# Idle TensorE products placed piece by piece in the PSUM tiles of an attention and MoE kernel

## The chip, the cores and the metric

The kernel runs on one core of a Trainium2 chip. The metric is device time in microseconds (us), the median of three runs. Five queues of instructions matter: TensorE (PE; its weight loads are PEld), VectorE (DVE), ScalarE (ACT), GpSimd (POOL) and SyncE (SP), which issues the DMAs. Each engine takes its instructions in the order in which the program lists them, and waits on semaphores that other engines count up.

## The reference

Eight batches of eight heads, 576 positions of 64 elements. For each head: `scores = q k^T / 8`, plus a decay that is the difference of cumulative sums of `log(clip(f))`, a causal mask, a softmax, and `attn @ v`. The heads of one position are then set side by side as 512 numbers (4608 tokens), and each token goes through `h = x @ w_in` (1024 wide), `solu = h * softmax(h)`, a layer norm scaled by `g_ln`, and `@ w_out` (back to 512). Everything is float32.

## The kernel before

Work goes by head pairs and halves of the positions (320 and 256), and by tiles of 128 tokens for the MoE part. For a pair, `scores` multiplies q and k into a `ps` tile (L519 plain float32 for the first batch's first half, L521 and L522 in split float32r pieces later), VectorE reduces it with the mask (L526), ScalarE takes the exponential (L529), GpSimd normalizes (L542), `transposes` turns the result on TensorE into `ps_t` (L568), which is copied out as `pth` (L295 on ScalarE, L297 on VectorE), and `values` multiplies with v into `ps_o` (L608). At the start, while the first batch runs, the weights are also unpacked from 8-byte words: `weights` uses a `ps_o` tile as scratch. ScalarE writes it (L376), VectorE combines bits in it (L379) and reads it into the weight buffer (L381).

PSUM is divided by `pool`: two tiles each of `ps`, `ps_t`, `ps_o` (in the listings below `ps_120`, `ps_121`, `ps_t_123`, `ps_t_124`, `ps_o_125`, `ps_o_126`). All instructions are first recorded as operations with a cost in ns and a due time. `Plan.schedule` then plays them through a model of the engines and gives each a planned start; the program is emitted in that order. The model also notes in `held`, for each PSUM tile, the planned spans in which it is taken.

Idle products come in at the emission. When the next planned operation is one of TensorE and starts later than TensorE is planned to be free, the loop at the end (L783 to L794) may put in products of the identity with itself (256 bf16 columns, L793), whose result nobody reads. The number is the planned gap less 100 ns, times 1.2, divided by the planned length of one. It does so only before 140 us of planned time, and only where `spare` finds a tile that is free through the whole planned gap.

Semaphores are set by program order: an instruction that writes a tile waits for every earlier listed instruction on another engine that reads or writes it. An idle product is listed right ahead of the TensorE operation that ends the gap, whatever planned time its tile was chosen for.

Of the kernel before, what the change touches and what calls it, by code (L numbers as in the profile page):

```python
# [37 lines left out]
COLUMN, TRANSPOSE = 0.4525, 109.0  # L38
# [1 line left out]

WI_H, WI_L, WO_H, WO_L = (1, 1, 1, 1), (3, 3, 2, 3), (2, 3, 2, 2, 3, 1, 1, 2), (2, 2, 2, 2, 2, 2, 2, 2)
P_32, X_32 = (1, 2, 1, 1), (2, 2, 2, 2, 1, 1, 1, 2)
FILLED, FILL = 140.0, 1.2
LANES = 8
WAIT = (0.0, 90.0, 60.0, 60.0, 0.0)


class Op:
# [3 lines left out]
class Plan:  # L52
# [30 lines left out]
    def schedule(self):  # L83
        free, wire, order, gone, self.held = [0.0] * 5, 0.0, [], {}, {}
        port, half_clock, worked, lanes = 0.0, True, 0.0, [0.0] * LANES
        todo = [[] for _ in range(5)]
        for o in self.ops:
            o.left, o.ready, o.users = len(o.deps), 0.0, []
            for d in o.deps:
                d.users.append(o)  # L90
            if not o.left:
                todo[o.eng].append(o)
        best = [None] * 5
        stale = set(range(5))
        for _ in self.ops:
            for e in stale:
                ready = []
                for o in todo[e]:
                    r = max(o.ready, free[e], port if o.port else 0.0)
                    if o.take:  # L100
                        if not self.pools[o.take[0]]:
                            continue
                        r = max(r, min(self.pools[o.take[0]])[0])
                    ready.append((r, o))
                best[e] = None
                if ready:
                    t = min(r for r, _ in ready) + WAIT[e]
                    best[e] = min((x for x in ready if x[0] <= t), key=lambda x: (x[1].due, x[1].seq))
            t, o = min((x for x in best if x), key=lambda x: x[0])
            stale = {PE, ACT, DVE, POOL, o.eng}  # L110
            todo[o.eng].remove(o)
            if o.take:
                place = min(self.pools[o.take[0]])
                self.pools[o.take[0]].remove(place)
                self.place[o.take] = place[1]
            if o.eng == SP:
                t = max(t, lanes.pop(0))
                free[SP] = t + 620.0
                wire = max(wire, t + 600.0) + o.ns
                o.end = max(t + 1900.0, wire + 1300.0)  # L120
                lanes.append(o.end)
            else:
                ns = o.ns
                if o.eng == PE:
                    if t < FILLED * 1e3:
                        half_clock = False
                    elif t - free[PE] > 1500.0:
                        half_clock, worked = True, 0.0
                    if half_clock:
                        ns *= 2.0  # L130
                        worked += ns if o.dense else 0.0
                        half_clock = worked < 3500.0
                free[o.eng] = t + ns
                o.end = t + ns
                if o.port:
                    port = o.end
                if o.tail:
                    wire = max(wire, t + 600.0)
                    o.end = max(t + o.tail, wire + 1300.0)
            after = AFTER[o.eng]  # L140
            for k in o.keys:
                gone[k] = max(gone.get(k, 0.0), o.end + after)
                self.uses[k] -= 1
                if not self.uses[k]:
                    self.pools[k[0]].append((gone[k], self.place[k]))
            for u in o.users:
                u.left -= 1
                u.ready = max(u.ready, o.end + (0.0 if u.eng == o.eng != SP else after + (90.0 if u.eng == PE else 0.0)))
                if not u.left:
                    todo[u.eng].append(u)  # L150
                    stale.add(u.eng)
            if o.take:
                self.held.setdefault((o.take[0], self.place[o.take]), []).append([t, 1.0e9])
            for k in o.keys:
                if not self.uses[k]:
                    self.held[k[0], self.place[k]][-1][1] = gone[k]
            order.append((t, o))
        return order

    def spare(self, a, e):  # L160

        for k, spans in self.held.items():
            if all(y <= a or x >= e for x, y in spans):
                return k

# [15 lines left out]
def tile_kernel(ctx: ExitStack, tc: tile.TileContext, qk, v, f, w_in, w_out, g_ln, out):  # L183
# [14 lines left out]
    plan = Plan(s=2, t=2, o=2)  # L198
# [585 lines left out]
    with tc.manual_schedule():  # L784
        busy = 3200.0
        for t, o in plan.schedule():
            if o.eng == PE:
                place = plan.spare(busy, t) if busy + 200.0 < t < FILLED * 1e3 else None
                if place:
                    p, n = place  # L790
                    dst = ps[n] if p == "s" else ps_o[n] if p == "o" else ps_t[n].rearrange("p c n -> p (c n)")
                    for _ in range(int(FILL * (t - busy - 100.0) / (256 * COLUMN))):
                        nc.tensor.matmul(dst[:, :256], blank[:, :P], blank, start=True, stop=True)  # L793
                busy = max(busy, o.end)  # L794
            o.fn()
# [40 lines left out]
```

## Time and profile before

| | us |
|---|---|
| median of 3 runs | 807.3 |
| lowest, highest | 806.41, 811.13 |
| the profiled execution | 804.66 |
| its span on the core | 802.8 |
| TensorE busy | 790.1 (98%) |
| mean granted TensorE clock | 0.994 |

Times in rows are us from the start of the span. A timeline row has start, length, engine, line, operation, out<-in, and in brackets the idle time of the engine just before with what ended it by the profile. Matmul rows overlap by their pipelined ends, so the distance from one start to the next is the cost of one. [...]

### The profile page before, as it was taken

To read this page: it belongs to the slowest core of one execution; us is meant where nothing else is said; L and a number is where in the kernel's file an instruction comes from. 1 tells how busy PE (TensorE), PEld (TensorE's weight loads), DVE (VectorE), ACT (ScalarE), POOL (GpSimd) and SP (SyncE) were. 2 spreads that over 40 slices of the span, in tenths; PEclk is the share of its full clock that TensorE was granted. 3 is DMA by queue.
4 is the path that set the end of the run, shared out by engine and by line. 5 is a ranking of instruction groups with operands and counts; after the bars stand their busy time and mean duration, and the time that the engine had idled before them with its cause. 6 is when DMAs were issued, how large, how long until landed. Compare 5 with 4: busy or idle time off the path is not lost.

```text
span 802.8 us, 15984 instructions
## 1 busy us (share of the span) xinstructions
PE 790.1 (98%) x4924; PEld 675.7 (84%) x4924; DVE 590.5 (74%) x1865; ACT 554.5 (69%) x1373; POOL 459.9 (57%) x668
## 2 busy tenths in 40 slices
PE   8799999999999999999999999999999999999998
PEld 6567889888888888888888888888888888888886
DVE  5698888987777787777777787777777787765233
ACT  6677588877777776777777776767777776764433
POOL 6476677876654565657555565657644656432230
PEclk9799999999999999999999999999999999999999
DMA  7767688886553554556544555555544554100000
GB/s 249 217 174 210 170 212 201 217 212 170 150 125 92 128 150 130 146 146 150 136 103 110 139 137 146 147 136 142 134 105 123 135 137 111 32 14 14 27 27 27
DMA packets 64213, 106.96 MB, mean 133 GB/s; under 512 B 11200, under 2 KB 25792, under 8 KB 63360
## 3 DMA queue, kind: packets, MB, share of 16 engines
q1 hardware_dynamic: 64128, 105.95, 50.1%
q8 instruction: 39, 0.64, 0.3%
q14 instruction: 46, 0.38, 0.2%
HBM read 39.11 MB, written 10.03 MB: 61 GB/s over the span
## 4 chain that ended last, share of the span: by engine, by line
PE 93%; DVE 2%; ACT 1%; DMA 1%; issue 1%; POOL 1%; SPq 0%; POOLq 0%; DVEq 0%; ACTq 0%
PE ps_o L608 15%; PE ps_t L568 11%; PE hps L648 8%; PE hps L649 8%; PE hps L650 8%; PE ps_o L703 8%; PE ps_o L704 8%; PE ps_o L705 8%; PE ps L521 6%; PE ps L522 6%; PE ps_t L692 4%; PE ps L793 2%; PE ps_t L793 1%; PE ps L519 1%; PE ps_o L793 1%
## 5 line engine op out<-in xcount | busy, mean ns | idle before, releaser
L542 POOL TENSOR_SCALAR p<-p,ri 64x64 f32<-64x64 f32 (+4 forms) x320 | 174.3, 558 | 123.4 <-DVE ri L538 53.4
L529 ACT ACTIVATE p<-p,nm 128x320 f32<-128x320 f32 (+4 forms) x320 | 178.9, 560 | 72.8 <-DVE nm L526 68.3
L576 DVE TENSOR_TENSOR ptl_f32r<-ps_t,pth_f32r 128x384 fp32r<-128x384 f32 (+3 forms) x272 | 138.9, 519 | 31.5 <-ACT pth_f32r L295 28.9
L526 DVE CUSTOM_DVE_ANT_0 p<-ps,mask 128x320 f32<-128x320 f32 (+4 forms) x320 | 132.7, 423 | 35.2 <-PE ps L522 21.5
L295 ACT ACTIVATE pth_f32r<-ps_t 128x384 fp32r<-128x384 f32 (+3 forms) x272 | 121.8, 461 | 34.3 <-PE ps_t L568 31.2
L568 PE MATMUL ps_t<-ident,p 128*128 128x128 f32 x800 | 130.9, 274 | 0.0
L648 PE MATMUL hps<-wi_h,xh 128*128 128x512 f32 x288 | 122.3, 425 | 0.0
L703 PE MATMUL ps_o<-wo_f32r,zh 128*128 128x512 f32 x280 | 118.5, 423 | 0.0
L568 PEld LDWEIGHTS ps_t<-ident,p 128*128 128x128 f32 x800 | 98.4, 140 | 23.5 <-issue 2.9
L650 PE MATMUL hps<-wi_h,xl 128*128 128x512 f32 x288 | 113.6, 394 | 0.0
L649 PE MATMUL hps<-wi_l,xh 128*128 128x512 f32 x288 | 113.6, 394 | 0.0
L704 PE MATMUL ps_o<-wo_f32r,zh 128*128 128x512 f32 x280 | 110.9, 396 | 0.0
L705 PE MATMUL ps_o<-wo_f32r,zl 128*128 128x512 f32 x280 | 110.2, 394 | 0.0
L521 PE MATMUL ps<-ks_f32r,qs_f32r 128*64 128x64 f32 (+2 forms) x360 | 107.5, 309 | 0.3 <-DVE nm L526 0.2
L522 PE MATMUL ps<-kz_f32r,qz 128*64 128x64 f32 (+2 forms) x360 | 104.1, 295 | 0.2
L608 PE MATMUL ps_o<-pth_f32r,vs_f32r 128*128 128x128 f32 (+1 forms) x368 | 96.1, 272 | 0.0
L644 POOL TENSOR_TENSOR xl<-xt,xh 128x512 fp32r<-128x512 f32 x36 | 47.5, 1318 | 70.0 <-ACT xh L643 65.9
L695 DVE TENSOR_TENSOR zl<-ps_t,zh 128x512 fp32r<-128x512 f32 x72 | 46.9, 686 | 53.2 <-ACT zh L694 52.6
L674 POOL TENSOR_SCALAR z<-e,st 128x1024 f32<-128x1024 f32 x35 | 41.0, 1172 | 70.2 <-ACT z L670 70.0
L521 PEld LDWEIGHTS ps<-ks_f32r,qs_f32r 128*128 128x128 f32 (+1 forms) x360 | 64.8, 180 | 10.8 <-DVE nm L526 2.7
L608 PE MATMUL ps_o<-ptl_f32r,vs_f32r 128*64 128x128 f32 (+1 forms) x368 | 71.2, 262 | 0.2 <-DVE ri L537 0.2
L608 PEld LDWEIGHTS ps_o<-pth_f32r,vs_f32r 128*128 128x128 f32 x368 | 69.3, 189 | 1.6
(126 smaller groups left out, 1612.2 us busy)
## 6 DMA issues: line engine op xcount, KB each, us to landing
raw<-in_qk_dram SPq DMA_DIRECT2D x64, 288.0 KB
ks_f32r<-hi SPq DMA_DIRECT2D x128, 144.0 KB
raw<-in_v_dram SPq DMA_DIRECT2D x32, 288.0 KB
kz_f32r<-raw SPq DMA_DIRECT2D x64, 144.0 KB
out_dram<-y SPq DMA_DIRECT2D x35, 256.0 KB
qs_f32r<-hi SPq DMA_DIRECT2D x56, 144.0 KB
qs_f32r<-raw SPq DMA_DIRECT2D x56, 144.0 KB
qz<-hi SPq DMA_DIRECT2D x56, 80.0 KB
```

The lines of the kernel that those rows point to most:

```text
L521: nc.tensor.matmul(dst, qs(p)[:, h, q0:q0 + nq], ks(p)[:, h, cols], start=True, stop=False)
L522: nc.tensor.matmul(dst, z[:, h, z0:z0 + nq], kz(p)[:, h, cols], start=False, stop=True)
L529: op(ACT, E_NS[i], at + 1.3, lambda: nc.scalar.activation(pr, pr, AF.Exp, bias=x, scale=-1.0, accum_out=sm[m][i][:nq, h, 0:1]), [("nm", m, ...
L542: op(POOL, N_NS[i], at + 2.8, lambda g=g, pg=pg: nc.gpsimd.tensor_scalar(pg, pg, r_[:, g:g + 1], 1.0, ALU.mult, ALU.mult), [("ri", m, i)], ...
L568: nc.tensor.transpose(tp[:, s, :], pt[i][:, k * P:(k + 1) * P], ident)
L608: nc.tensor.matmul(o[:mm, a:w], vv, mv, start=(j == 0 and x == 0), stop=(j == order[-1] and x == 0))
L648: nc.tensor.matmul(hps[:, sl], xh[:, c, :], wi_h[:, c, sl], start=(c == 0), stop=False)
L649: nc.tensor.matmul(hps[:, sl], xh[:, c, :], wi_l[:, c, sl], start=False, stop=False)
L650: nc.tensor.matmul(hps[:, sl], xl[:, c, :], wi_h[:, c, sl], start=False, stop=(c == NCC - 1))
L703: nc.tensor.matmul(o, zh[a][:, j], wo(0, k), start=(k == 0), stop=False)
L704: nc.tensor.matmul(o, zh[a][:, j], wo(1, k), start=False, stop=False)
L705: nc.tensor.matmul(o, zl[a][:, j], wo(0, k), start=False, stop=(k == NFC - 1))
```

## The change

The two constants become a table of stretches of planned time with a share each: up to 140 us (1.2) and from 690 us on (0.8). `spare` becomes a generator. It walks through the gap, takes at each point the tile that stays free longest from there, yields the piece, and goes on from where that tile's next span begins. The loop fills each piece.

```diff
-FILLED, FILL = 140.0, 1.2
+FILLED = ((0.0, 140.0, 1.2), (690.0, 1000.0, 0.8))
+def share(t):
+
+    return next((x for a, e, x in FILLED if a <= t / 1e3 < e), 0.0)
...
-                    if t < FILLED * 1e3:
+                    if share(t):
                         half_clock = False
...
     def spare(self, a, e):
 
-        for k, spans in self.held.items():
-            if all(y <= a or x >= e for x, y in spans):
-                return k
+        while a < e:
+            free = {k: min([x for x, _ in spans if x > a] + [e]) for k, spans in self.held.items() if not any(x <= a < y for x, y in spans)}
+            if free:
+                k = max(free, key=free.get)
+                yield k, a, free[k]
+                a = free[k]
+            else:
+                a = min(y for spans in self.held.values() for _, y in spans if y > a)
...
-                place = plan.spare(busy, t) if busy + 200.0 < t < FILLED * 1e3 else None
-                if place:
-                    p, n = place
+                for (p, n), x, y in plan.spare(busy + 100.0, t) if busy + 200.0 < t and share(t) else ():
                     dst = ps[n] if p == "s" else ps_o[n] if p == "o" else ps_t[n].rearrange("p c n -> p (c n)")
-                    for _ in range(int(FILL * (t - busy - 100.0) / (256 * COLUMN))):
+                    for _ in range(int(share(t) * (y - x) / (256 * COLUMN))):
                         nc.tensor.matmul(dst[:, :256], blank[:, :P], blank, start=True, stop=True)
```

The order of VectorE, ScalarE, GpSimd and SyncE is the same in both programs, and so is that of TensorE's other products. The idle products go from 292 to 346. Three batches are new (45, 5 and 4 products) and one of 15 moves from `ps_t_124` to `ps_120`. Line numbers behind the change are 8 to 10 higher.

The first place is TensorE at the batch of 45, between the last scores of a pair in the first stage and the values of the pair before it. Before the change (names in brackets are the semaphores that an instruction waits for; DMAHW stands for DMA queues):

```order
L519 MATMUL ps_120<-kz_k,qs_q 128x320 [waits DVE_49]
L519 MATMUL ps_121<-kz_k,qs_q 128x320 [waits DVE_49]
L608 MATMUL ps_o_125<-pth_f_366,raw_75 64x320 [waits DMAHW1_49,DVE_49,Activation_49]
L608 MATMUL ps_o_125<-pth_f_366,raw_75 64x128
L608 MATMUL ps_o_125<-pth_f_366,raw_75 64x256
L608 MATMUL ps_o_126<-pth_f_366,raw_75 64x320 [waits DVE_49]
```

With the change, 23 products in `ps_o_125` and 22 in `ps_120` stand there:

```order
L529 MATMUL ps_120<-kz_k,qs_q 128x320 [waits DVE_49]
L529 MATMUL ps_121<-kz_k,qs_q 128x320 [waits DVE_49]
L801 LDWEIGHTS ident
L801 MATMUL ps_o_125<-ident 128x256 [waits DVE_49]
...
L801 MATMUL ps_120<-ident 128x256
...
L618 MATMUL ps_o_125<-pth_f_366,raw_75 64x320 [waits DMAHW1_49,Activation_49]
L618 MATMUL ps_o_125<-pth_f_366,raw_75 64x128
```

The wait on VectorE has moved from the values to the first idle product; the values keep the two others. What VectorE does on `ps_o_125` there is the same in both programs (rows of before):

```order
L379 SCALAR_TENSOR_TENSOR ps_o_125<-ptl_w,ps_o_125 128x512 [waits Activation_49]
L381 SCALAR_TENSOR_TENSOR ptl_w<-wo_raw,ps_o_125 128x512 [waits DVE_49]
L379 SCALAR_TENSOR_TENSOR ps_o_126<-e,ps_o_126 128x512 [waits Activation_49]
L381 SCALAR_TENSOR_TENSOR e<-wo_raw,ps_o_126 128x512 [waits DMAHW2_49,DVE_49]
L392 TENSOR_TENSOR wi_l<-ptl_w,wi_h 128x1024 [waits Activation_49]
L526 ISA p_69,nm_81<-ps_120,mask 64x64 [waits PE_49]
```

Nothing moved here. The second row is the last that touches `ps_o_125` ahead of the values; the last row waits for TensorE's next scores.

The second place is the batch of 5 on TensorE at the end of the first stretch, ahead of values in `ps_o_126`. Before:

```order
L521 MATMUL ps_120<-ks_f32r,qs_f32r 64x64 [waits DMAHW6_49,DMAHW7_49,DMAHW5_49,DMAHW2_49]
L522 MATMUL ps_120<-kz_f32r,qz_63 64x64 [waits DMAHW7_49,DMAHW0_49]
L608 MATMUL ps_o_126<-pth_f32r,v_0_1_66 128x320 [waits DVE_49,Activation_49]
L608 MATMUL ps_o_126<-ptl_f32r,v_0_1_66 64x320 [waits DVE_49]
L793 LDWEIGHTS ident
L793 MATMUL ps_t_123<-ident 128x256
```

With the change:

```order
L531 MATMUL ps_120<-ks_f32r,qs_f32r 64x64 [waits DMAHW6_49,DMAHW7_49,DMAHW5_49,DMAHW2_49]
L532 MATMUL ps_120<-kz_f32r,qz_63 64x64 [waits DMAHW7_49,DMAHW0_49]
L801 LDWEIGHTS ident
L801 MATMUL ps_o_126<-ident 128x256 [waits DVE_49]
...
L618 MATMUL ps_o_126<-pth_f32r,v_0_1_66 128x320 [waits Activation_49]
L618 MATMUL ps_o_126<-ptl_f32r,v_0_1_66 64x320 [waits DVE_49]
```

Again the wait on VectorE has moved to the first of the five.

## Rows read from the trace of the kernel before

**Rows 1.** The page: busy time by engine, and TensorE's clock in 40 slices.

```profile
PE 790.1 (98%) x4924; PEld 675.7 (84%) x4924; DVE 590.5 (74%) x1865; ACT 554.5 (69%) x1373; POOL 459.9 (57%) x668
...
PEclk9799999999999999999999999999999999999999
```

**Rows 2.** Waits of TensorE in the whole span: waiting line, releaser, total, times, longest.

```profile
PE ps_o L608 <- ACT pth_f L295: 4.6, 1, 4.6
PE ps L793 <- POOL ident masks.py:199: 3.4, 1, 3.4
PE ps_o L716 <- ACT zh L694: 0.5, 1, 0.5
PE ps L521 <- DVE nm L526: 0.2, 1, 0.2
PE ps_o L608 <- DVE ri L537: 0.2, 1, 0.2
```

**Rows 3.** Windows around the gap: length, TensorE busy (instructions), clock, DMA share, GB/s.

```profile
24.58:27.99 3.41, 1.59 (x9) 1.00 0.88 210
27.99:30.73 2.74, 0.00 (x1) 0.50 0.41 110
30.73:35.08 4.35, 4.35 (x9) 0.50 0.90 293
35.08:38.23 3.15, 3.15 (x14) 0.50 0.93 327
38.23:42.00 3.77, 3.77 (x28) 1.00 0.26 78
```

**Rows 4.** Timeline of TensorE through the gap and behind it.

```profile
24.93 1.24 PE L519 MATMUL ps<-kz_k,qs_q 65*128 65x320 f32 x4
30.73 4.02 PE L608 MATMUL ps_o<-pth_f,raw 64*64 64x320 f32 x8 [4.55 <-ACT pth_f L295]
...
35.08 0.69 PE L519 MATMUL ps<-ks_k,vs_q 65*64 65x64 f32 x4
```

**Rows 5.** Timeline of ScalarE and of VectorE in the gap, and TensorE's queue (L608, min/median/max ns).

```profile
29.66 0.48 ACT L295 ACTIVATE pth_f<-ps_t 128x384 f32<-128x384 f32 x1
...
29.94 0.69 DVE L381 SCALAR_TENSOR_TENSOR ptl_w<-wo_raw,ps_o 128x512 int32<-128x512 int32 x1
...
L608 PEldq EVENT_SEMAPHORE  x1: 5602/5602/5602, 25.1 to 25.1; - x1
```

**Rows 6.** Windows of the idle products (L793) alone: length, PE busy (count), PEld busy.

```profile
3.42:7.51 4.09, 4.09 (x20) 2.90 (x21) 1.00 0.86 304
7.51:11.29 3.78, 3.78 (x35) 3.21 (x33) 1.00 0.38 85
```

**Rows 7.** Timeline of VectorE behind the gap.

```profile
35.60 0.22 DVE L526 CUSTOM_DVE_ANT_0 p<-ps,mask 64x64 f32<-64x64 f32 x1 [2.50 <-PE ps L519]
...
37.67 0.16 DVE L538 RECIPROCAL ri<-ri 64x2 f32<-64x2 f32 x1
38.59 0.36 DVE L526 CUSTOM_DVE_ANT_0 p<-ps,mask 128x192 f32<-128x192 f32 x1 [0.76 <-PE ps L519]
```

**Rows 8.** Timelines at the batch of 5: VectorE, then TensorE.

```profile
149.62 0.43 DVE L631 TENSOR_TENSOR xt<-ps_o,tm 64x256 f32<-64x256 f32 x1
150.08 0.56 DVE L576 TENSOR_TENSOR ptl_f32r<-ps_t,pth_f32r 128x384 fp32r<-128x384 f32 x1
...
150.20 0.39 PE L608 MATMUL ps_o<-pth_f32r,v 128*128 128x320 f32 x1
150.69 0.36 PE L608 MATMUL ps_o<-ptl_f32r,v 128*64 128x320 f32 x1
```

**Rows 9.** Timeline of TensorE at the batch of 4, in the last tile.

```profile
791.86 1.03 PE L692 MATMUL ps_t<-ident,z 128*128 128x128 f32 x8
793.41 0.39 PE L716 MATMUL ps_o<-wo_f32r,zh 128*128 128x256 f32 x1 [0.52 <-ACT zh L694]
```

**Rows 10.** Timelines at the batch of 15 that moves: VectorE, then TensorE.

```profile
80.47 0.44 DVE L526 CUSTOM_DVE_ANT_0 p<-ps,mask 128x288 f32<-128x288 f32 x1
80.83 0.08 DVE L526 DVE_READ_ACCUMULATOR2_ANT nm<- 128x1 f32 x1
...
80.97 1.81 PE L793 MATMUL ps_t<-ident 128*128 128x256 bf16 x15
82.54 0.30 PE L608 MATMUL ps_o<-pth_f32r,vs_f32r 128*128 128x128 f32 x1
```

## The prediction, made before the changed kernel had run

> **What bounds the kernel now.** I read the page first: TensorE is busy for 98% of the span, all other engines 74% or less, and its clock is whole in every slice but the second [rows 1]. So a microsecond that TensorE gains or loses lasts to the end unless a wait takes it up. The list of TensorE's waits comes next. It holds one wait of 4.6 us ahead of the values L608, one at the start that the change does not touch, and 0.9 us in all after that [rows 2]. The windows around the long wait show what else it costs: the scores end at 26.17, the gap lasts to 30.73, the clock drops to 0.50 at 27.99 and is back at 1.00 only at 38.23 [rows 3, 4]. From 30.73 to 38.23, 7.50 us, real products run without a pause at the low clock [rows 3]. At full clock they would need 3.75 us, so at most 3.75 us of speed and 4.55 us of idle time are to be had here. No other stretch shows a low clock.
>
> **What releases the gap.** The wait list names ScalarE's L295, but that copy ended at 29.66 + 0.48 = 30.14, 0.59 us before the values start [rows 5]. The queue row says more: TensorE's sequencer stood 5.60 us in one semaphore instruction of L608, from 25.1 to 30.7 [rows 5]. VectorE's L381, which reads `ps_o_125` as scratch of the weights, ended at 29.94 + 0.69 = 30.63 [rows 5]; 0.1 us later the values write that tile. The wait that ends last is thus the one on VectorE.
>
> **The 45 products.** In the changed order the first of them writes the same `ps_o_125` and carries a wait on VectorE, and the values, which had such a wait, have none left. That can only be if the idle product's wait covers theirs: it waits for L381 as well. The planner chose the tile because it is free early in the gap, before the scratch use begins; but the products are listed at the end of the gap, behind that scratch use, and the waits follow the list. I therefore expect the gap to stay as it is, 4.55 us, the clock to fall as it does now, and 45 products to run from about 30.7 ahead of the values.
>
> Their price. After the pause at the start the same products ran 20 in 4.09 us, then 35 in 3.78 us [rows 6]: 0.205 us each at the low rate, 0.108 at the full one. Taking the same run-up, 20 products take 4.1 us and the other 25 take 2.7 us: **6.8 us added**. The bounds are 45 x 0.108 = 4.9 us and 45 x 0.205 = 9.2 us. I take 6.8 because this batch is the same instructions in an unbroken row after a pause, which is just what the start shows.
>
> [...]
>
> What it gives back. By 37.5 the clock is up, so the products that ran at 0.50 from 30.73 to 38.23 now run at 1.00. The first 4.35 us, to the scores at 35.08, have no late partner left after a delay of 6.8 us: they need half, **2.2 us less**. In the other 3.15 us VectorE sets a floor. It stood idle for 2.50 us until these scores [rows 7], and its row is blocked behind them in either program. From its first reduction at 35.60 to the end of L538 at 37.83 it needs 2.2 us, and the next reduction, at 38.59, cannot start before that. At full clock TensorE would bring the scores for it 1.6 us sooner, VectorE is ready 38.59 - 37.83 = 0.76 us sooner plus about 0.3 us that the first scores end earlier. I take **1.1 us less**. Together 3.3, with bounds 2.2 (the second part gives nothing) and 3.75 (half of all).
>
> **The batch of 5.** Its wait is on VectorE too, and again the values lose theirs. The last reader of `ps_o_126` is L631, ended 150.05; the values start at 150.20 [rows 8]. So five products, 0.54 us, again come behind the wait. The second values product starts 0.49 us after the first, at 150.69, just after VectorE's L576 ended at 150.64 [rows 8], while 320 columns at the full rate of rows 6 take about 0.14 us (320 x 0.108 / 256) [rows 6]; so some 0.35 us of that distance was a wait, which the five products now fill. **0.2 us added**, bounds 0 and 0.54.
>
> **The batch of 4.** It takes 0.43 us where TensorE waits 0.52 us for ScalarE [rows 9], and its tile `ps_120` is not in use by then: **nothing added**; without that cover it would be 0.43. The clock is at 1.00 there [rows 1], so there is nothing to restore.
>
> **The batch of 15** has the same count. It now follows VectorE's read of `ps_120`, which ends at 80.91, and its products start at 80.97 [rows 10]: nothing, at worst the 0.1 us by which that read could be late.
>
> **Who else waits.** While TensorE is 6.8 us later, VectorE stands before the scores L519 with its whole row behind it, ScalarE behind VectorE, GpSimd behind both; nobody holds work that TensorE later needs sooner. DMAs are not moved. After 38 us TensorE has 0.9 us of waits [rows 2] to take up a delay, and they are on VectorE and ScalarE, which are as late.
>
> **Sum:** +6.8 - 3.3 + 0.2 = **+3.7 us**. The profiled execution took 804.66 us, so 808.4 by its own time; the median of the runs shown is 807.3, 2.6 higher, and gives **811.0**. The bounds add to 4.9 - 3.75 = +1.1 and 9.2 - 2.2 + 0.54 + 0.43 = +8.0.
>
> **Rivals.**
>
> 1. *It works as meant, and the kernel gets faster.* If the first idle product waited for an older use of `ps_o_125`, the products would start at 26.2, and 45 x 0.108 = 4.9 us would end at 31.1, 0.4 later than the values start now. The clock would stay at 1.00 and the 7.50 us would shrink by 3.3 to 3.75. That is -3.3 + 0.4 + 0.2 = -2.7: 804.6. It decides at whether the products run before 30.6. For it: the whole price of the gap is in the rows. Against it: the values have lost their wait. Chance 0.08. [...]
>
> 2. *The delay is given back.* TensorE's row behind 38 us holds idle products whose count stays, but the waits that they cover are on VectorE, which is late as well. Only what DMAs release could be ready sooner: they run at a share of 0.90 to 0.93 from 30.73 to 38.23 [rows 3] and would go on through the delay. Giving back 2 to 3.7 us leads to 807.3 to 809. Against it: TensorE waits for no DMA after the gap [rows 2]. Chance 0.12.
>
> 3. *The clock stays low for longer.* After the gap, 7.50 us of real products went by before it rose [rows 3]. If that holds for the idle products, 36.6 of them take 7.5 us and 8.4 take 0.9: 8.4 - 3.3 + 0.2 = +5.3, 812.6. If all 45 and part of the values run low, 9.2 - 2.2 + 0.2 = +7.2, or 814.5 and more. For it: this is the nearest row in place. Against it: those were small float32 products, these are the ones of the start. Chance 0.14, a third of it above 814.5.
>
> My forecast has the other 0.66.
>
> **Range and chances.** The range leaves out rival 1, the end of rival 2 and that of rival 3: 807.0 to 814.5. A measurement of this kernel tells about 1% (8 us) from no change. Faster by that much would need 799.2, which no case gives: 0.02. Slower needs 815.4: the upper end of rival 3 and what I have missed, 0.08. Within 1%: 0.90.
>
> **What would show it.** In the changed profile: TensorE's wait of about 4.5 us stays, but ahead of an idle product in `ps_o`, with VectorE's L391 (L381 before) ending just before it; the 45 products start near 30.7, not 26.2; the low clock begins near 28 as now and ends some 4 us after the products begin; the values start near 37.5 and the stretch that took 7.50 us takes about 4.2; the five products near 153 to 154 follow L641. What would make me wrong: products that start at 26.2 with a clock of 1.00 throughout (rival 1), a last tile that ends at the old time in spite of late values (rival 2), or a low clock beyond the batch (rival 3).

## The result, and the profile after

The changed kernel took 812.92 us (median of 15 runs, 808.72 to 816.0) against 808.0 for the kernel before (15 runs, 806.41 to 811.13): ratio 1.0056, 95% interval 1.0042 to 1.007, which is +4.5 us (+3.4 to +5.7). The forecast was +3.7 us, within 1%. The execution that was profiled here is the slowest of the 15, at 816.0, for a reason shown below.

TensorE's waits in the changed kernel (waiting line, releaser, total, times, longest), which answer to [rows 2]:

```profile
PE ps_o L801 <- DVE ptl_w L391: 4.5, 1, 4.5
PE ps L801 <- POOL ident masks.py:199: 3.4, 1, 3.4
PE ps_o L618 <- ACT pth_f L305: 1.8, 1, 1.8
PE ps L532 <- DMA kz_f32r<-raw: 1.3, 3, 0.6
PE ps_o L618 <- DVE xt L641: 0.7, 1, 0.7
PE ps L532 <- DMA qz<-hi: 0.5, 1, 0.5
```

The wait of 4.5 us is still there. It now stands ahead of an idle product in `ps_o`, and the profile names VectorE's L391 (L381 in the kernel before) as its end. The first of the four rows under the start's wait has the names of the gap's row in [rows 2], but is another wait, near 64 us; the other three are not in [rows 2], and the one on `L716` in the last tile is gone from the list.

The timeline of TensorE at the gap, against [rows 4]:

```profile
24.95 1.24 PE L529 MATMUL ps<-kz_k,qs_q 65*128 65x320 f32 x4
30.67 4.69 PE L801 MATMUL ps_o<-ident 128*128 128x256 bf16 x23 [4.48 <-DVE ptl_w L391]
35.20 2.57 PE L801 MATMUL ps<-ident 128*128 128x256 bf16 x22
37.70 2.22 PE L618 MATMUL ps_o<-pth_f,raw 64*64 64x320 f32 x8
```

The products do not run in the gap. They start where the values started before, and the values follow 7.0 us later. VectorE's row that they waited for ended at 29.94 + 0.69 = 30.63:

```profile
29.94 0.69 DVE L391 SCALAR_TENSOR_TENSOR ptl_w<-wo_raw,ps_o 128x512 int32<-128x512 int32 x1
```

The windows of the same execution, against [rows 3] (length, then busy time of PE, PEld, DVE, ACT and POOL with the instructions, TensorE's granted clock as a share of the full one, DMA share, GB/s):

```profile
28.02:30.67 2.65, 0.00 (x0) 0.00 (x0) 1.75 (x5) 2.11 (x6) 2.65 (x3) 0.50 0.58 155
30.67:34.85 4.18, 4.18 (x20) 2.90 (x20) 2.38 (x3) 1.06 (x1) 0.85 (x2) 0.50 0.67 250
34.85:37.70 2.85, 2.85 (x28) 2.34 (x25) 0.00 (x0) 0.00 (x0) 0.00 (x0) 1.00 0.99 373
37.70:42.00 4.30, 4.30 (x24) 2.43 (x24) 1.46 (x8) 1.26 (x6) 0.00 (x0) 1.00 0.11 40
...
65.57:72.39 6.82, 6.82 (x21) 3.53 (x22) 3.94 (x10) 3.82 (x9) 2.64 (x5) 0.50 0.78 273
```

20 products ran at the low clock in 4.18 us, the others at the full one in 2.85, and the real products behind them start at full clock. The third window also shows the price outside TensorE: VectorE, ScalarE and GpSimd did nothing at all. VectorE stood 7.39 us behind the scores that TensorE had not yet made, ScalarE 8.97 us behind VectorE, GpSimd 10.93 us behind TensorE's transposes:

```profile
40.48 0.22 DVE L536 CUSTOM_DVE_ANT_0 p<-ps,mask 64x64 f32<-64x64 f32 x1 [7.39 <-PE ps L529]
```

The last row of the windows is a second stretch at 0.50, which [rows 1] do not have: it follows the 1.8 us wait near 64 us, which ended at 64.00. It belongs to single executions, as far as the mean clocks tell (one of them has a trace): of 27 timed runs of this kernel in two sets, 5 had a mean clock of 0.992 or less and took 814.4 to 817.5 us, where the others had 0.995 or 0.996; 3 of 35 runs of the kernel before had 0.985 and took 814.5 to 814.9.

**Where the time went.** For each profile, when a given real product of TensorE started, less when it started in the first profile of the kernel before (worked out from the starts in both traces; columns are by the time in that first profile):

| kernel | 24.4 | 45.6 | 65.1 | 150.1 | last product |
|---|---|---|---|---|---|
| before, 2nd profile | -0.13 | +1.41 | +1.40 | +3.30 | +3.36 |
| before, 3rd profile | +0.31 | +2.06 | +2.60 | +2.65 | +2.93 |
| changed, 1st profile | +0.02 | +3.63 | +8.66 | +10.77 | +11.34 |
| changed, 2nd profile | +0.58 | +4.49 | +5.95 | +8.57 | +9.63 |
| changed, 3rd profile | +0.59 | +4.54 | +5.54 | +8.80 | +9.48 |
| changed, 4th profile | -0.09 | +3.48 | +4.13 | +5.84 | +7.16 |
| without the 45 | +0.79 | +1.12 | +2.65 | +2.96 | +4.00 |
| 20 behind the wait | +0.80 | +2.06 | +2.03 | +3.62 | +5.09 |
| 90 behind the wait | +0.06 | +8.61 | +8.61 | +10.14 | +11.02 |
| 46 in `ps_120` | -0.51 | -3.13 | -2.23 | -0.98 | 0.00 |
| 39 in `ps_120` alone | -0.02 | -3.39 | -3.40 | -2.09 | +1.09 |
| second piece (22) alone | +0.90 | +0.56 | +0.55 | +2.46 | +4.00 |

Less what the start differs, the four profiles of the changed kernel are +3.61, +3.91, +3.95 and +3.57 at 45.6 us; the sum had +3.5 for that place. Against the other two profiles of the kernel before they are only 1.8 to 2.4 us later there, because the low clock at the gap lasted 13.65 us in those two, against 10.24 (last section). Nothing comes back from there to the end. All profiles lose something more on the way, those of the kernel before too: the first profile, on which the forecast rested, was the fastest execution of the kernel before that any set had (804.66; the lowest of the 35 in the next set is 804.70).

### The profile page after: what moved, and what is told of

Read it like the earlier page. It is cut to its first block, busy times and chain, and to the rows that moved or that the text cites. A ratio compares the mean times of both kernels' runs of the same rounds, so it can differ in the third digit from the quotient of the medians.

```text
span 814.1 us, 16091 instructions
## 1 busy us (share of the span) xinstructions
PE 797.9 (98%) x4978; PEld 681.6 (84%) x4978; DVE 592.4 (73%) x1865; ACT 553.4 (68%) x1373; POOL 458.3 (56%) x668
## 4 chain that ended last, share of the span: by engine, by line
PE 88%; DVE 5%; DMA 2%; ACT 2%; issue 1%; POOL 1%; SPq 0%; DVEq 0%; POOLq 0%; ACTq 0%
PE ps_o L618 13%; PE ps_t L578 10%; PE hps L658 8%; PE hps L660 8%; PE hps L659 8%; PE ps_o L713 8%; PE ps_o L714 7%; PE ps_o L715 7%; PE ps L532 5%; PE ps L531 5%; PE ps_t L702 4%; PE ps L801 2%; DVE p L536 1%; PE ps_o L801 1%; DVE ptl_f32r L586 1%; DMA ptl_raw<-in_w_out_dram 1%
## 5 line engine op out<-in xcount | busy, mean ns | idle before, releaser
L532 PEld LDWEIGHTS ps<-kz_f32r,qz 128*128 128x128 f32 (+1 forms) x360 | 65.2, 181 | 8.5 <-issue 1.3
```

Of the source, the lines that this page charges most:

```text
L532: nc.tensor.matmul(dst, z[:, h, z0:z0 + nq], kz(p)[:, h, cols], start=False, stop=True)
```

## The experiments

Each was timed against the kernel before on the same chip, but for the four single profiles at the end. Brackets behind a ratio are its 95% interval.

**The changed kernel once more** (no edit).

> The changed kernel once more, for a second profile. My theory (the 45 products wait for VectorE's L391 and run behind the gap): wait of about 4.5 us ahead of the products, values at 37.7, a shift of +3.6 us against before from 40 us on. The profile of the first look had +1.9 us from a late DMA at 64 us and a second low-clock stretch at 65.57 to 72.39. If those belong to that one execution, this profile lacks the second low clock and its span is about 3 us shorter; the rival, that they belong to the change, has both again (span about 814). Time: +4 to +5 us against before.

812.62 us (12 runs) against 807.29 (35 runs): ratio 1.0061 (1.0036 to 1.0087). The profile has the wait of 4.5 us, the products behind it, and no second low clock: its span is 812.4, not 814.1, so 1.7 us shorter where about 3 was expected. The late load of `w_out` is there again, so it was not settled whether that belongs to the change; the four profiles at the end of this section return to it.

**Without the 45.** The batches of 5 and 4 and the moved 15 stay.

```diff
-... in plan.spare(busy + 100.0, t) if busy + 200.0 < t and share(t) else ():
+... in plan.spare(busy + 100.0, t) if busy + 200.0 < t and share(t) and not 22.0e3 < busy < 23.0e3 else ():
```

> The change without its batch of 45; the batches of 5 and 4 and the moved 15 stay. My theory: nearly all of the price is the 45, so +0.2 us against before (0 to +0.5), and in the profile a step of about +0.2 at 150 us and none at the last tile. Rival: the three small edits cost a good part of the +4.9, then +1 to +2.

807.39 us against 807.29: ratio 0.9999 (0.9974 to 1.0024). The 45 products are the price; the three small edits cost nothing that can be measured, though the interval reaches up to +1.9 us. The profile's step at 150 us is +0.08 (from +2.96 to +3.04) where +0.2 was expected, and there is none at the last tile.

**The same place, another tile.** 46 products, all in `ps_120`.

```diff
+first = 22.0e3 < busy < 23.0e3 and busy + 200.0 < t
-for (p, n), x, y in plan.spare(busy + 100.0, t) if ...
+for (p, n), x, y in [(("s", 0), busy + 100.0, t)] if first else plan.spare(busy + 100.0, t) if ...
```

> The same place in TensorE's row, 46 idle products, all in ps_120, whose last reader (VectorE's L536 of the first scores) ended at 26.3 us; the values keep their own wait for VectorE's L391. My theory (what decides is which earlier work the tile makes the products wait for): products start at 26.3 to 26.4, end near 31.4, no low clock from 28 to 38, values 0.6 us later than in before, the 7.5 us of real work behind them shrink by 3.3 to 3.75: -2.7 + 0.2 = -2.5 us against before. Rival (idle products ahead of the values only cost their own time, wherever they wait): +2 or more.

805.28 us against 807.29: ratio 0.997 (0.9944 to 0.9997), -2.4 us; the forecast for it was -2.5. It is the one version here whose interval lies wholly under that of no change. Its timeline at the gap and a window over it (columns as above):

```profile
25.83 5.18 PE L802 MATMUL ps<-ident 128*128 128x256 bf16 x46 [0.16 <-DVE nm L536]
30.94 2.22 PE L618 MATMUL ps_o<-pth_f,raw 64*64 64x320 f32 x8
```

```profile
25.83:30.94 5.11, 5.11 (x47) 4.40 (x46) 3.67 (x11) 4.54 (x11) 4.11 (x5) 1.00 0.63 148
30.94:37.81 6.87, 6.87 (x40) 4.33 (x40) 5.56 (x19) 4.09 (x12) 1.71 (x4) 1.00 0.98 341
```

The products wait 0.16 us in place of 4.48, the gap is filled and the clock is at 1.00 throughout; ScalarE and GpSimd work through the gap as before (busy for 4.54 and 4.11 of its 5.11 us here, for 3.98 and 3.38 of 4.56 from 26.17 to 30.73 in the kernel before). The place in the order is the same, the number nearly so, only the tile differs. That settles what the products waited for, and that idle products cost their time where they come after the wait and not where they run in the gap (the 46 overran it: less what the start differs, the values are 0.7 us later than before).

**20 products behind the wait**, in `ps_o_125` alone.

```diff
+for (p, n), x, y in [(("o", 0), t - 1980.0, t)] if first else plan.spare(...) ...
```

> 20 idle products in ps_o_125 in place of 45; they wait for VectorE's L391 as the 45 do. My theory: 20 at the low rate take 4.1 us, the clock rises at about their end, the real work saves 3.3: +4.1 - 3.3 + 0.2 = +1.0 us against before. Rival (what raises the clock is the whole batch, or the delay by itself triggers late DMAs): values run low for some us more, +2 to +4.5.

808.87 us (12 runs) against 807.29: ratio 1.0012 (0.9993 to 1.0032), +1.0 us by the ratio and +1.6 by the medians; +1.0 was expected. The interval, -0.6 to +2.6, holds both no change and the lower end of the rival, so the profile has to tell. The 20 took from 31.46 to 35.81, 4.35 us; the clock rose at 36.48, 0.67 us into the values behind them, and not some us later as the rival has it:

```profile
31.46 4.42 PE L802 MATMUL ps_o<-ident 128*128 128x256 bf16 x20 [4.48 <-DVE ptl_w L391]
35.81 2.54 PE L618 MATMUL ps_o<-pth_f,raw 64*64 64x320 f32 x8
```

8 values products take 2.54 us here and 4.02 in [rows 4].

**90 products behind the wait.**

```diff
+for (p, n), x, y in [(("o", 0), t - 8700.0, t)] if first else plan.spare(...) ...
```

> 90 idle products in ps_o_125 in place of 45, behind the same wait; the rest as in the change. My theory (products behind the wait are paid in full and nothing is given back later): 45 more at the full rate, 0.109 us each, +4.9 us on top of the change's measured +4.9 to +5.3, so +8.6 (from the predicted +3.7) to +10.2 against before. Rival (a delay here is given back by DMAs and by the waits that idle products cover): clearly less than +4.9 on top, +5 to +7 in all.

816.29 us (6 runs) against 807.72: ratio 1.0101 (1.0083 to 1.0119), +8.2 us (+6.7 to +9.6). That is 3.3 to 3.7 us above the changed kernel's +4.5 and +4.9, less than the 4.9 that 45 products take at full clock; the total is 0.4 under the lower end of what I expected, and over the rival's +7. The interval of the time alone would not part the theory from the rival. In its profile the delay is +8.61 at 45.6 us and still +8.61 at 65.1, 4.6 to 5.0 more than in the changed kernel less what the starts differ, so the products are paid in full at their place:

```profile
30.71 12.04 PE L802 MATMUL ps_o<-ident 128*128 128x256 bf16 x90 [4.48 <-DVE ptl_w L391]
42.68 1.54 PE L618 MATMUL ps_o<-pth_f,raw 64*64 64x320 f32 x6
```

**The change with its second piece alone**: the 22 in `ps_120` stay, the 23 in `ps_o_125` go.

```diff
-... in plan.spare(busy + 100.0, t) if busy + 200.0 < t and share(t) else ():
+... in [k for k in plan.spare(busy + 100.0, t) if not first or k[0][0] == "s"] if busy + 200.0 < t and share(t) else ():
```

> The change without its first piece (23 in ps_o_125); its second piece (22 in ps_120) stays, and so do the batches of 5 and 4. My theory: the 22 wait only for the first scores' reduction, start at 26.3 in before's time and end at 28.7, so about 2 us of idle time are left until VectorE's L391 ends. The values start when they do in before. If the clock holds over the rest of the gap: -3.3 + 0.2 = -3.1 us against before; if it falls all the same: +0.2, as without the 45. I take the first as likelier (0.6), since the longest idle row is then less than half of before's. The rival of the whole account, that products cost their time wherever they stand, has +2.4.

808.06 us against 807.72: ratio 1.0001 (0.9979 to 1.0023). I had thought the other outcome likelier. The windows show why it fails (columns as above):

```profile
27.23:29.80 2.57, 2.56 (x22) 2.05 (x21) 1.50 (x7) 2.57 (x8) 1.56 (x3) 1.00 0.60 163
29.80:31.60 1.80, 0.00 (x1) 0.03 (x1) 1.49 (x3) 1.22 (x4) 1.80 (x2) 1.00 0.29 56
31.60:33.24 1.64, 1.64 (x7) 0.75 (x8) 1.61 (x3) 1.05 (x1) 0.81 (x2) 1.00 0.91 365
33.24:40.07 6.83, 6.83 (x26) 4.49 (x25) 4.51 (x17) 3.50 (x10) 1.65 (x3) 0.50 0.80 275
```

The clock is whole through the 1.80 us that stay idle, and falls 1.64 us after real work has begun again; then 6.83 us run at 0.50. Of 12 runs 11 have a mean clock of 0.996 or less; the one with 1.0 took 802.88.

**39 products in `ps_120`, nothing else of the change**, in the kernel before.

```diff
-place = plan.spare(busy, t) if busy + 200.0 < t < FILLED * 1e3 else None
+first = 22.0e3 < busy < 23.0e3 and busy + 200.0 < t
+place = ("s", 0) if first else plan.spare(busy, t) if busy + 200.0 < t < FILLED * 1e3 else None
...
-for _ in range(int(FILL * (t - busy - 100.0) / (256 * COLUMN))):
+for _ in range(39 if first else int(FILL * (t - busy - 100.0) / (256 * COLUMN))):
```

> The kernel before with one batch added: 39 products in ps_120 at this gap, nothing else of the change. My theory: products from 26.3 to about 30.6, values no later than in before, the clock at 1.00 throughout, the real work behind saves 3.3 to 3.75: -3.5 us against before, 0.7 to 1.0 us better than the 46 in ps_120. Rival (the gap's filler gains only part, the rest goes to later waits on DMAs): -2 or less, no better than the 46.

806.09 us against 807.72: ratio 0.9982 (0.9964 to 1.0), -1.5 us, no better than the 46. In its profile the gap went as I thought: the values start at 30.71 and are 3.4 us ahead by 45.6.

```profile
26.32 4.42 PE L794 MATMUL ps<-ident 128*128 128x256 bf16 x39 [0.16 <-DVE nm L526]
30.71 2.19 PE L608 MATMUL ps_o<-pth_f,raw 64*64 64x320 f32 x8
```

But against the first profile of the kernel before it keeps nothing of that to the last product (+1.09; against the other two it ends 2.4 and 1.5 us ahead), so the -3.5 was missed and the rival's number came true. Of the 4.5 us lost behind 45.6 us, 1.8 are waits on DMAs. And of its 12 runs 5 have a mean clock of 0.996 or less, where of the 46 it is 2 of 12. Where the clock fell in those five isn't seen, as only one execution has a trace.

**Four more profiles**, two of each kernel.

> The kernel before, one more profile. Open is whether the wait of 1.4 to 1.8 us ahead of the values near 64 us, behind a late load of w_out (8.3 to 8.8 us from issue to ScalarE's use, in both profiles of the change; 6.0 in the one of before), belongs to the change. Theory: it is a draw of the execution, so it shows up in one or two of four further profiles, in before as likely as after. Rival: the delay puts the load against other DMAs, so both profiles of the change have it and both of before lack it.

> The kernel before once more, for the time of the w_out load (6.0 us or 8 and more) and the wait behind it. Theory and rival as for the first of these four looks.

> The changed kernel, one more profile: 45 products behind a wait of 4.5 us, shift of +3.6 us against before at 45 us (less what the start differs), and the w_out load at 6 us (theory: half of the time) or at 8 and more (rival: again).

> The changed kernel once more, for the time of the w_out load and the wait behind it: 6 us in at least one of the two looks by the theory, 8 and more in both by the rival.

The kernel before took 808.04 and 807.6 us, the changed one 814.15 and 811.82. From the issue of that load to ScalarE's use of it: kernel before 6.0, 5.7 and 7.4 us; changed 8.8, 8.3, 7.8 and 7.5; without the 45, 8.4; with 20, 5.7; with 90, 5.6; with the 46 in `ps_120`, 7.7; with the 39 and with the second piece alone, 5.7. The wait of TensorE behind it was 1.8, 1.4, 0.9 and 0.6 in the four of the changed kernel, 0.5 (5.0 less the gap's 4.5) in the third profile of the kernel before, 1.5 (6.0 less 4.5) without the 45, and 0.8 with the 46, where TensorE is ahead by then. So it comes without a delay as well, and not always with one; but all four of the changed kernel have it, and neither my reading nor the rival's is shown. The fourth profile of the changed kernel has these waits:

```profile
PE ps_o L801 <- DVE ptl_w L391: 4.5, 1, 4.5
...
PE ps L532 <- DMA kz_f32r<-raw: 1.1, 3, 0.6
PE ps_o L618 <- DVE xt L641: 0.7, 1, 0.7
PE ps_o L618 <- ACT pth_f L305: 0.6, 1, 0.6
...
PE ps L532 <- DMA qz<-hi: 0.3, 1, 0.3
```

The waits on DMAs do divide the kernels. In total from 40 us on, by the list of each profile: 0, 0.2 and 0 us in the kernel before, 0 without the 45; 1.8, 1.4, 2.0 and 1.4 in the changed one, 1.9 with 20, 1.3 with 90, 1.6 and 1.8 with the 46 and the 39 in `ps_120`, 1.5 with the second piece alone.

## Why the prediction was right

**The wait.** It held that the gap stays because the tile, not the planned time, sets the wait. The profile names VectorE's L391, the products start at 30.67, and with `ps_120` in place of `ps_o_125` the same products start 0.16 us after the scores. The mechanism is shown. Rival 1 (it works as meant) is out for the changed kernel, and its price came out near for the version that does it, -2.4 measured and -2.7 worked out, though in part by luck (below).

**The 45.** 6.8 us by the run-up of the start; 7.03 measured (30.67 to 37.70), with 20 at the low rate, as taken. (In [rows 6] a clock of 1.00 stands beside the first 20 products of the start too, because that trace has no clock entry before 7.51; their low rate is read from the 0.205 us each.) Rival 3, that the clock stays low through the batch, is out: it rose 4.18 us after the first product.

The number of slow products differs between profiles of the changed kernel: 20 of the 45 ran slow in the first and 23 in the second. From the first product to full clock it was 4.18 us in the first profile and 4.79 in the second (31.23 to 36.02), and the values then came 7.03 and 7.32 us after the first product. In the fourth they came 6.97 us after it (30.57 to 37.54). The second profile's window, of the idle products alone (columns as in [rows 6]):

```profile
31.23:36.02 4.79, 4.79 (x23) 3.42 (x23) 0.50 0.89 331
```

**What it gives back.** 3.3 us worked out; TensorE's shift fell from +6.97 at the values (37.70 against 30.73) to +3.57 at the scores that were at 38.28, 3.4 us. The total fits, its parts do not. The shift is +5.03 at the scores that were at 35.08, so the first part gave 1.94 in place of 2.2, and the second 1.46 in place of 1.1, nearly half of its 3.15. The floor that VectorE was to set did not hold TensorE up: from VectorE's first reduction to the next it took 1.75 us (40.48 to 42.23) in place of the 2.99 in [rows 7], and TensorE has no wait between 37.8 and 60 us. That two misses of 0.3 us cancel is luck.

```profile
42.23 0.36 DVE L536 CUSTOM_DVE_ANT_0 p<-ps,mask 128x192 f32<-128x192 f32 x1
```

**The small batches.** The 5 were to add 0.2. In the changed kernel the two values products stand 0.22 us apart in place of the 0.49 of [rows 8], so the wait between them is now filled. The scores behind them that were at 151.38 come 0.24 us less late than the ones ahead of the batch (+10.53 against +10.77). So this term had the wrong sign in the changed kernel, where TensorE waits 0.46 us for a DMA just ahead of the batch, and was too large without the 45 (+0.08). The 4 in the last tile fill ScalarE's wait exactly:

```profile
803.20 1.03 PE L702 MATMUL ps_t<-ident,z 128*128 128x128 f32 x8
804.07 0.60 PE L801 MATMUL ps<-ident 128*128 128x256 bf16 x4
804.75 0.39 PE L726 MATMUL ps_o<-wo_f32r,zh 128*128 128x256 f32 x1
```

From the transposes to the products it is 1.55 us here and 1.55 in [rows 9].

**What the sum lacked.** It had +3.7; the two sets measured +4.5 (3.4 to 5.7) and +4.9 (2.9 to 7.0). Up to 45.6 us the terms fit to 0.1 to 0.5 us, against the profile from which they were worked out. Against the other two profiles of the kernel before, what the batch gives back was 1.5 to 1.8 us too small, since there was more low clock to save. What is missing comes behind 45.6 us: from there to the last product the four profiles of the changed kernel lose 3.7 to 7.7 us and the three of the kernel before 0 to 2.0, where the sum had nothing. As far as three profiles stand for the kernel before, the two errors have opposite signs, and it is in part luck that +3.7 lies so near the measured time. The same holds for the -2.4 of the 46 products: at 45.6 us that profile is ahead of the three of the kernel before by 2.6, 4.2 and 4.4 us; at the last product it is 0.5 behind the first and 3.0 and 2.1 ahead of the others.

Rival 2 asked only whether some of the delay would be given back; it is out, as no profile of the changed kernel comes nearer behind 45.6 us. "Who else waits" took a late TensorE to be late by the same amount everywhere, and the DMAs not to be moved. They are moved: a load that SyncE issues behind the gap goes out 4.2 us later (first row before, second changed).

```profile
37.08 0.33 SPq L301 DMA_DIRECT2D raw<-in_qk_dram  x1
41.24 0.33 SPq L311 DMA_DIRECT2D raw<-in_qk_dram  x1
```

Part of the loss is 1.4 to 2.0 us of waits on DMAs from 40 us on, which the profiles of the kernel before lack (0 to 0.2), and 0.6 to 1.8 us behind the load of `w_out`. The waits on DMAs come with every version in which some real work behind the gap runs at full clock, with the values late (20, 45, 90) or not late (39, 46), and not in the one without the 45, where that work runs at 0.50 as in the kernel before (8.36 us, 31.49 to 39.85, against 7.50). So it does not take a delay to bring them. They are not the whole loss: without the 45 TensorE loses 2.9 us behind 45.6 us with none of them. That the loads for the next pairs, issued from the work behind the gap, are not ready for a TensorE that goes through it about 3 us faster would fit twelve of the thirteen profiles. With the second piece alone TensorE has only gained 0.3 us by 45.6 us (at most 1.4 on the way), and waits 1.5 us for DMAs all the same. This was argued and not tried; the cause stays open.

## What to carry to other kernels

In these runs an idle product waited for every earlier listed use of the tile it writes: at the same place 4.48 us in `ps_o_125` and 0.16 us in `ps_120`. Where filler is chosen by planned time but listed at the end of a gap, a tile that is free now and taken later in the same gap is a bad choice: take the one whose last listed use ends first, or a tile that nothing else touches yet. Before timing such a change, look in the listing for the wait that moved from the real instruction to the filler. And a filler that leaves part of a gap open can lose the clock all the same, later than the gap: with 22 products and 1.80 us left open it fell 1.64 us behind the gap.

## What the runs showed of the hardware that I had not expected

With the second piece alone the clock fell after the idle time was over: 1.64 us into real work, behind 1.80 us of idle time that itself ran at 1.00, and 6.83 us at 0.50 followed. The first profile of the changed kernel has the same once more: a wait of 1.82 us ended at 64.00, and the clock fell at 65.57, 1.57 us into real work.

```profile
64.00 1.54 PE L618 MATMUL ps_o<-pth_f,raw 64*64 64x320 f32 x6 [1.82 <-ACT pth_f L305]
```

In three profiles of the kernel before, the same gap cost 10.24, 13.65 and 13.65 us of low clock (27.99 to 38.23, 27.73 to 41.38, 28.62 to 42.27; the mean clocks are 0.994, 0.991 and 0.992), so one trace of such a stretch is one draw: the one that the forecast used was the cheapest of the three.
